# Norm products of q and k with a stationary tile of 128 columns in place of one of 16

## The chip, the cores and the metric

The kernel runs on one core of one Trainium2 chip. The metric is device time in microseconds, the median of repeated executions. TensorE is called PE below (PEld is its loading of stationary tiles), VectorE is DVE, ScalarE is ACT, GpSimd is POOL; SP is the engine whose queue issues nearly all DMAs here.

## The reference

Two kinds of layer alternate, attention (A) and a gated linear unit (B), twice each with the same weights, on x of 2048 tokens by 448 features; all is float32.

```python
def _A_ref(x, wqkv, wo):                 # H = 16 heads of Dh = 28
    qkv = transpose((x @ wqkv).reshape(B, S, 3, H, Dh), 2, 0, 3, 1, 4)
    q, k, v = qkv[0], qkv[1], qkv[2]
    scores = einsum("bhqd,bhkd->bhqk", q, k) * (Dh ** -0.5)
    o = einsum("bhqk,bhkd->bhqd", softmax(scores), v)
    return transpose(o, 0, 2, 1, 3).reshape(B, S, D) @ wo
def _B_ref(x, w_gate, w_up, w_down):     # F = 1792
    return (sigmoid(x @ w_gate) * (x @ w_up)) @ w_down

x = x + _A_ref(layernorm(x), wqkv, wo)
x = x + _B_ref(layernorm(x), w_gate, w_up, w_down)
x = x + _A_ref(layernorm(x), wqkv, wo)
x = x + _B_ref(layernorm(x), w_gate, w_up, w_down)
```

## The kernel before

The order of the instructions on every engine is the order in which the program writes them; no scheduler moves anything. x stays in SBUF. Products with weights are made of f16 parts: each float32 operand is split into a high and a low part, and a product is the sum of high by high, high by low and low by high.

Each of the two layers runs through projection, attention, output projection and gated unit. The change lies in the projection (`project`), which goes over four blocks of 512 tokens: for each block `qk` and then the values (`vals`); the blocks 2 and 3 have their `qk` first and their values after.

`qk(b, ...)` makes the 896 rows of q and k in seven tiles of 128 rows. For each tile i, eleven matmuls of 512 columns go into a PSUM bank (`by_features`, L362). ACT scales the sum to f16 (L506), DVE takes the low part (L507), ACT squares the high part into the bf16 tile `sq` (L509), DVE takes the larger of its first and second half of the columns (L511), SP stores both parts to DRAM (L514). Between these, the list `fill` gives each tile a piece of preparation for later blocks: layer norm, transposes on DVE, stores and gathers through DRAM (`store` L269, `gather` L277), splits into parts (`ready`, L172, L173, L177, L178). In layer 0 the weights are scaled and split along with the first block (`along`, L185, L188), and block 1 is transposed on PE (`turn`, L328) instead of through DRAM.

The norm products bound the scores. `ind` is a table of 8 tiles of [128, 16] in bf16: entry (p, i, h) is 1 where row p of a tile of q or k belongs to head h, else 0; the first four entries of i serve the tiles 0 to 3 for q, the second four the tiles 3 to 6 for k. A matmul of 256 columns with `ind[:, i, :]` as its stationary tile sums the squares of each head into 16 rows of a PSUM bank, `qnorm` for i up to 3 (L485) and `knorm` for i from 3 on (L488); the tile i = 3 holds rows of both and has two products. `sq` of tile i is not used at once: the products wait in `late` until two more tiles have had their matmuls, so those of tile 0 come after the matmuls of tile 2, and the last two tiles' products come in `finish`, which the code calls in the values that follow or in the next block. DVE then takes the largest of each head's row (L524, `peaks`). After block 3 a bound for every head comes of `peaks`, and from it a row that is added to the scores, and a flag (`guard_of_norms`, `worst_of_heads`).

Attention then works in tiles of 32 stationary columns at four places of the array (L821, L839). `ind` is written once at the start: POOL makes it in float32 (L150 to L156) and DVE copies it to bf16 (L159).

Of the kernel before, what the change touches and what calls it, by code (L numbers as in the profile page):

```python
# [12 lines left out]
BF16 = mybir.dt.bfloat16  # L13
# [6 lines left out]
P = 128  # L20
S = 2048
D = 448
H = 16
# [5 lines left out]
W = TB * P  # L29
# [54 lines left out]
def interleaved_layers(ctx: ExitStack, tc: tile.TileContext, x_in, wqkv, wo, w_gate, w_up,  # L84
                       w_down, out):
    nc = tc.nc
    ctx.enter_context(tc.manual_schedule())

    cpool = ctx.enter_context(tc.tile_pool(name="cpool", bufs=1))
# [26 lines left out]
    def bank(i, name):  # L116
        return psum(f"bank{i}", name, [P, 512])
# [4 lines left out]
    half = cpool.tile([P, 8], F32, name="half")  # L122
    nhalf = cpool.tile([P, TB], F32, name="nhalf")
    ind_f = qrt.get("ind_f", [P, 8, H])
    ind = cpool.tile([P, 8, H], BF16, name="ind")
    warm = cpool.tile([P, 1], F32, name="warm")

    ones = cpool.tile([P, P], F32, name="ones")
# [22 lines left out]
    for j in range(2):  # L151
# [4 lines left out]
        nc.gpsimd.affine_select(out=v, in_=v, compare_op=ALU.is_ge, fill=0.0,  # L156
                                base=DH - 1 - off, pattern=[[-P, 4], [DH, H]],
                                channel_multiplier=-1)
    nc.vector.tensor_copy(ind, ind_f)  # L159
    qrt.put(ind_f)  # L160


# [187 lines left out]
    def by_features(pm, blk, wh, wl, first_tile=None):  # L350

        order = [(wh, blk.hi), (wh, blk.lo), (wl, blk.hi)]
        terms = [(w(kt), x[:, kt, :]) for kt in range(3) for w, x in order]
        tails = [(w(3), blk.tail) for w in (wh, wl)]
        if first_tile == 0:
            terms = terms[0::3] + terms[2::3] + terms[1::3] + tails
        elif first_tile == 1:
            terms = terms[0::3] + terms[1::3] + tails[0:1] + terms[2::3] + tails[1:2]
        else:
            terms += tails  # L360
        for i, (w, x) in enumerate(terms):
            nc.tensor.matmul(pm, w, x, start=(i == 0), stop=(i == len(terms) - 1))  # L362
# [104 lines left out]
    def project(layer, wq, first):  # L467
# [11 lines left out]
        def qk(b, blk, fill, before):  # L479
            pn = [bank(4 + 2 * (b % 2), "qnorm"), bank(5 + 2 * (b % 2), "knorm")]  # L480
            late = deque()

            def norm_products(i, sq):
                if i <= 3:
                    nc.tensor.matmul(pn[0][0:H, 0:W // 2], ind[:, i, :], sq[:, 0:W // 2],  # L485
                                     start=(i == 0), stop=(i == 3))
                if i >= 3:
                    nc.tensor.matmul(pn[1][0:H, 0:W // 2], ind[:, 1 + i, :], sq[:, 0:W // 2],  # L488
                                     start=(i == 3), stop=(i == 6))
                qrt.put(sq)  # L490

            for i in range(7):
                pm = bank(evac[0] % 4, "qkp")
                evac[0] += 1
                c = slice(i * P, (i + 1) * P)
                by_features(pm, blk, lambda kt: wq.qk[0][:, kt, c],
                            lambda kt: wq.qk[1][:, kt, c], i if layer == 0 and b == 0 else None)
                if layer == 0 and b == 0:
                    along[i]()
                if i == 1 and before:  # L500
                    before()
                if len(late) == 2:
                    late.popleft()()
                hl = qrt.get("qkhl", [P, 2, W], F16)
                sq = qrt.get("sq", [P, W], BF16)
                nc.scalar.activation(hl[:, 0, :], pm, AF.Copy, scale=PS)  # L506
                nc.vector.scalar_tensor_tensor(hl[:, 1, :], pm, PS, hl[:, 0, :], op0=ALU.mult,  # L507
                                               op1=ALU.subtract)
                nc.scalar.activation(sq, hl[:, 0, :], AF.Square)  # L509

                nc.vector.tensor_tensor(sq[:, 0:W // 2], sq[:, 0:W // 2], sq[:, W // 2:W],  # L511
                                        op=ALU.max)
                n = slice(b * W, (b + 1) * W)
                nc.sync.dma_start(qk_scr[c, :, n], hl)  # L514
                qrt.put(hl)
                late.append(lambda i=i, sq=sq: norm_products(i, sq))
                if i < len(fill) and fill[i]:
                    fill[i]()

            def finish():  # L520
                while late:
                    late.popleft()()
                for i in range(2):
                    nc.vector.tensor_reduce(peaks[:, i, b:b + 1], pn[i][0:H, 0:W // 2], axis=AX.X,  # L524
                                            op=ALU.max)
            return finish
# [38 lines left out]
        sq = lambda b, *js: lambda: blks[b].squares(js)  # L565
# [19 lines left out]
        else:  # L585
# [4 lines left out]
            along_values = {0: b2.store, 3: lambda: b1.ready(3),  # L590
                            2: lambda: (b1.ready(0, 1, 2), fin(), b2.gather())}
        fin = qk(0, blks[0], fill, None)
        vals(0, blks[0], along_values)
        if layer == 0:
            fill = [b2.gather, b3.norm, sq(3, 0, 1), sq(3, 2, 3), idle,
                    lambda: b2.ready(0, 1), lambda: (b2.ready(2, 3), b3.store())]
        else:
            fill = [idle, b3.norm, lambda: b2.ready(0, 1), lambda: b2.ready(2, 3), sq(3, 0, 1),
                    sq(3, 2, 3), b3.store]
        fin = qk(1, b1, fill, None)  # L600
        vals(1, b1, {0: b3.gather, 1: fin})
        fin = qk(2, b2, [idle, lambda: b3.ready(0, 1), lambda: b3.ready(2, 3)], None)
        fin = qk(3, blks[3], [], fin)
        if layer > 0:
# [515 lines left out]
```

## Time and profile before

| | |
|---|---|
| three runs | 2023.3, 2023.67, 2027.02 us; median 2023.67 us |
| the profiled execution | 2026.13 us |
| its span, from the first to the last instruction | 2024.2 us |
| granted PE clock, mean | 0.998 |
| projection of layer 0 / layer 1 | about 17 to 129 us / 1020 to 1129 us of the span |
| norm products in the profile | 64, in 48 places of PE's stream |

A row of the time order reads: start in us, busy time in us, engine, line, operation, output<-inputs, shape of the stationary tile (rows\*columns), shape of the moving data and type, how many of them were merged; in brackets the idle time of the engine before it and what ended that. A row of a stretch reads: start:end, its length, then busy time and (xinstructions) of PE, PEld, DVE, ACT and POOL, the granted clock, the DMA share and GB/s. A row of a group reads: line, engine, operation, output<-inputs, shapes, count, then busy time in us, mean ns of one, idle time before them and what ended it. A row that gives durations as three numbers has least/median/most in ns. In the chain of work that ended last a row has start, time, engine, tile, line and count. SPq is the issuing queue of SP. Matmuls overlap, and their ends are modelled, so that distances are best taken from start to start.

### The profile page before, as it was taken

What the parts mean: (1) busy time and instruction counts of PE and PEld (TensorE: products, weight loads), DVE (VectorE), ACT (ScalarE), POOL (GpSimd) and SP (SyncE); (2) the same over time, 40 slices, a digit from 0 to 9 for tenths busy, and PEclk for the clock granted to TensorE, in tenths of its full rate; (3) what the DMA queues carried; (4) which work ended last, traced back from release to release, by engine and by line L of the source; (5) the groups of instructions that cost most, each with busy time, mean ns of one, the idle gap of its engine ahead of it and who ended that gap; (6) DMA issues with size and microseconds to landing.
All of it is one profiled execution on the core that took longest, in us unless ns stands there. A gap on an engine that the chain in (4) does not pass through costs nothing. (4 is left out here: it accounts for less than half of the span.)

```text
span 2024.2 us, 47829 instructions
## 1 busy us (share of the span) xinstructions
PE 2005.5 (99%) x21637; PEld 1028.8 (51%) x21637; DVE 748.8 (37%) x1110; ACT 1189.6 (59%) x1136; POOL 33.3 (2%) x75
## 2 busy tenths in 40 slices
PE   8999999999999999999999999999999999999999
PEld 4445555555554444444444555555555544444444
DVE  6635455551235232323274133222322432323222
ACT  5469999999961212121244799999999412121211
POOL 2000000000000000000000000000000000000000
PEclk9999999999999999999999999999999999999999
DMA  4563454741215100001143221121202250101000
GB/s 164 156 195 96 130 157 147 227 131 30 57 59 188 37 13 25 19 19 33 59 130 120 66 66 34 42 46 30 66 12 63 68 204 1 55 1 55 1 19 19
DMA packets 98630, 153.75 MB, mean 76 GB/s; under 512 B 9584, under 2 KB 79216, under 8 KB 95600
## 3 DMA queue, kind: packets, MB, share of 16 engines
q1 hardware_dynamic: 89728, 146.21, 23.9%
q10 hardware_dynamic: 8688, 4.36, 0.8%
q8 instruction: 174, 2.85, 0.6%
q14 instruction: 40, 0.33, 0.1%
HBM read 97.52 MB, written 45.68 MB: 71 GB/s over the span
## 5 line engine op out<-in xcount | busy, mean ns | idle before, releaser
L828 ACT ACTIVATE prob_s<-sc 128x1536 f32<-128x1536 f32 (+1 forms) x684 | 918.2, 1509 | 2.6 <-PE sc L821 1.4
L839 PE MATMUL acc<-prob_s,val_s 128*32 128x256 f32 x8192 | 571.7, 379 | 0.0
L821 PE MATMUL sc<-qp_s 114*32 114x512 f16 x8192 | 569.8, 380 | 1.5 <-ACT val_s L537 1.3
L362 PEld LDWEIGHTS <-gu_s 128*128 128x128 f16 x2464 | 241.1, 98 | 290.4 <-issue 6.4
L839 PEld LDWEIGHTS acc<-prob_s,val_s 128*32 128x32 f32 x8192 | 273.6, 110 | 179.8 <-ACT prob_s L828 0.4
L821 PEld LDWEIGHTS <-qp_s 114*32 114x32 f16 x8192 | 245.8, 95 | 222.3 <-issue 75.8
L362 PE MATMUL gate<-xhl_s,gu_s 128*128 128x512 f16 x1232 | 285.1, 379 | 4.2 <-ACT xhl_s L172 2.6
L362 PE MATMUL up<-xhl_s,gu_s 128*128 128x512 f16 x1232 | 284.2, 379 | 0.0
L1028 ACT ACTIVATE sig_q<-gate 128x512 f32<-128x512 f32 x112 | 66.9, 597 | 341.0 <-PE gate L362 324.8
L1033 DVE SCALAR_TENSOR_TENSOR sig_q<-up,sig_q 128x512 f32<-128x512 f32 x112 | 77.5, 692 | 460.9 <-PE up L362 460.9
L172 ACT CAST hhl_q<-sig_q 128x512 f16<-128x512 f32 x112 | 69.3, 618 | 288.1 <-DVE sig_q L1033 288.1
L853 DVE COPY oraw_q<-acc 128x512 f32<-128x512 f32 x32 | 22.1, 692 | 484.5 <-PE acc L839 484.4
L999 PE MATMUL dnp<-dn_s,hhl_q 128*128 128x448 f16 x448 | 157.9, 352 | 0.0
L998 PE MATMUL dnp<-dn_s,hhl_q 128*128 128x448 f16 x448 | 157.9, 352 | 0.0
L1000 PE MATMUL dnp<-dn_s,hhl_q 128*128 128x448 f16 x448 | 157.9, 352 | 0.0
L362 PE MATMUL qkp<-xhl_s,wqk_s 128*128 128x512 f16 x616 | 140.8, 380 | 0.9 <-DVE xhl_s L178 0.7
L855 DVE RECIPROCAL oden_q<-oden_q 128x512 f32<-128x512 f32 x32 | 107.3, 3353 | 1.1
L173 DVE TENSOR_TENSOR hhl_q<-sig_q,hhl_q 128x512 f16<-128x512 f32 x112 | 77.5, 692 | 76.7 <-ACT hhl_q L172 76.7
L362 PEld LDWEIGHTS <-wqk_s 128*128 128x128 f16 x616 | 57.2, 98 | 71.7 <-issue 4.5
L506 ACT ACTIVATE qkhl_q<-qkp 128x512 f16<-128x512 f32 x56 | 33.4, 596 | 65.5 <-PE qkp L362 65.4
L999 PEld LDWEIGHTS <-hhl_q 128*128 128x128 f16 x448 | 43.8, 98 | 43.8
L998 PEld LDWEIGHTS <-hhl_q 128*128 128x128 f16 x448 | 43.8, 98 | 43.8
(113 smaller groups left out, 1034.8 us busy)
## 6 DMA issues: line engine op xcount, KB each, us to landing
qp_s<-qk_scr SPq DMA_DIRECT2D x96, 224.0 KB
qk_scr<-qkhl_q SPq DMA_DIRECT2D x56, 256.0 KB
gu_s<-gu_parts SPq DMA_DIRECT2D x14, 1024.0 KB
xraw_s<-xt_scr SPq DMA_DIRECT2D x14, 768.0 KB
xt_scr<-xs_s SPq DMA_DIRECT2D x38, 224.0 KB
qp_s<-qk_scr SPq DMA_DIRECT2D x64, 112.0 KB
gu_parts<-pack_s SPq DMA_DIRECT2D x7, 1024.0 KB
raw_s<-in_B_w_down_dram SPq DMA_DIRECT2D x6, 896.0 KB
```

Source lines behind the costliest of these rows:

```text
L172: nc.scalar.copy(hi, raw)
L173: nc.vector.tensor_tensor(lo, raw, hi, op=ALU.subtract)
L362: nc.tensor.matmul(pm, w, x, start=(i == 0), stop=(i == len(terms) - 1))
L821: nc.tensor.matmul(ps[32 * j:32 * j + 32, a, :], hd.k[:, keys], hd.q[:, qb * W:(qb + 1) * W], start=True, stop=True, tile_position=(0, 32 ...
L828: nc.scalar.activation(prob[:, 0:n, :], ps[:, 0:n, :], AF.Exp, scale=exp_scale)
L839: nc.tensor.matmul(acc[qb * VC:(qb + 1) * VC, n], v[:, kc % TB, h, :], probs[c * NB + qb][:, n], start=(kc == 0 and i % 2 == 0), stop=(kc ...
L855: nc.vector.reciprocal(den, den)
L998: nc.tensor.matmul(pm, hl[:, 0, s], dw[:, 0, :], start=(f == 0), stop=False)
L999: nc.tensor.matmul(pm, hl[:, 0, s], dw[:, 1, :], start=False, stop=False)
L1000: nc.tensor.matmul(pm, hl[:, 1, s], dw[:, 0, :], start=False, stop=(f == NF - 1))
L1028: nc.scalar.activation(sig, pgu[0], AF.Sigmoid, scale=gate_scale)
L1033: nc.vector.scalar_tensor_tensor(sig, pgu[1], PS, sig, op0=ALU.mult, op1=ALU.mult)
```

## The change

`ind` gets seven more tiles of zeros behind its eight (POOL writes them at the start). The norm products take as their stationary tile the 128 columns that begin at tile i of the table, which are tiles i to i+7, in place of the 16 columns of tile i. They write 128 rows of the PSUM bank in place of 16. The first 16 rows are what was written before; the other 112 are sums over other tiles' heads, which nobody reads. The products are the same in number, place and moving data, and `peaks` still reads the first 16 rows. In the changed file the products stand at L490 and L493, the other lines of `project` move down by five.

```diff
-    ind = cpool.tile([P, 8, H], BF16, name="ind")
+    ind = cpool.tile([P, 7 + P // H, H], BF16, name="ind")
...
-    nc.vector.tensor_copy(ind, ind_f)
+    nc.gpsimd.memset(ind[:, 8:, :], 0.0)
+    nc.vector.tensor_copy(ind[:, 0:8, :], ind_f)
...
+            def rows_of_heads(i):
+
+                return ind[:, i:i + P // H, :].rearrange("p a h -> p (a h)")
+
             def norm_products(i, sq):
                 if i <= 3:
-                    nc.tensor.matmul(pn[0][0:H, 0:W // 2], ind[:, i, :], sq[:, 0:W // 2],
+                    nc.tensor.matmul(pn[0][:, 0:W // 2], rows_of_heads(i), sq[:, 0:W // 2],
                                      start=(i == 0), stop=(i == 3))
                 if i >= 3:
-                    nc.tensor.matmul(pn[1][0:H, 0:W // 2], ind[:, 1 + i, :], sq[:, 0:W // 2],
+                    nc.tensor.matmul(pn[1][:, 0:W // 2], rows_of_heads(1 + i), sq[:, 0:W // 2],
                                      start=(i == 3), stop=(i == 6))
                 qrt.put(sq)
```

## The prediction

> **What bounds the kernel now.** I read the page's busy shares first, then the stretches, the waits of PE, the order of time on PE and PEld around the products that change, and last what holds PE before and after them. The stretches are cut at the ends of the stages: layer 0's projection is the second row, layer 1's the third.
>
> ```profile
> span 2024.2 us, 47829 instructions
> ...
> PE 2005.5 (99%) x21637; PEld 1028.8 (51%) x21637; DVE 748.8 (37%) x1110; ACT 1189.6 (59%) x1136; POOL 33.3 (2%) x75
> 17.00:131.00 114.00, 111.21 (x556) 49.80 (x555) 69.08 (x142) 56.94 (x94) 6.50 (x10) 1.00 0.42 129
> 1020.00:1129.00 109.00, 106.84 (x508) 46.34 (x507) 63.54 (x134) 50.07 (x85) 5.89 (x8) 1.00 0.44 135
> ```
>
> PE is busy for 111.2 of 114 us and 106.8 of 109 us there, at the full granted clock (the 1.00): what leaves PE's stream shortens the span, unless PE must then wait. But busy hides gaps between pipelined matmuls, so I take the price of a product from starts, not durations.
>
> ```profile
> 100.84 2.55 PE L362 MATMUL qkp<-xhl_s,wqk_s 128*128 128x512 f16 x11
> 103.31 0.28 PE L485 MATMUL qnorm<-sq_q,ind 128*16 128x256 bf16 x1
> 103.52 2.55 PE L362 MATMUL qkp<-xhl_s,wqk_s 128*128 128x512 f16 x11
> 106.00 0.28 PE L485 MATMUL qnorm<-sq_q,ind 128*16 128x256 bf16 x1
> 106.21 2.55 PE L362 MATMUL qkp<-xhl_s,wqk_s 128*128 128x512 f16 x11
> 108.69 0.28 PE L485 MATMUL qnorm<-sq_q,ind 128*16 128x256 bf16 x1
> 108.80 0.27 PE L488 MATMUL knorm<-sq_q,ind 128*16 128x256 bf16 x1
> 109.01 2.55 PE L362 MATMUL qkp<-xhl_s,wqk_s 128*128 128x512 f16 x11
> ...
> 100.83 2.06 PEld L362 LDWEIGHTS <-wqk_s 128*128 128x128 f16 x11
> 103.31 0.09 PEld L485 LDWEIGHTS <-ind 128*16 128x16 bf16 x1 [0.42 <-issue]
> ...
> 1629.53 2.37 PE up L362 x11
> 1631.90 2.37 PE gate L362 x11
> ```
>
> Eleven 512-column matmuls with nothing between take 2.37 us (the last two rows, from the chain in order of time). Two products that follow each other stand 0.11 us apart (108.69 to 108.80). So eleven matmuls and one product should take 2.48 us. From 100.84 to 106.21 two such rounds take 5.37 us, 2.685 each: about 0.205 us more per visit. Of it some 0.10 us is on the way out: from 103.31 to 103.52 is 0.21, not 0.11; the rest is on the way in. The PEld rows show the same thing: among equal tiles a stationary load runs ahead of its matmul, but the load of `ind` starts in the instant its matmul starts, 0.42 us after the load before it. PE is emptied ahead of the product and once more behind it. A visit with two products pays this once: there are 64 products (32 of L485, 32 of L488), 16 visits hold two, so 48 visits, 24 in each layer.
>
> **The change, part by part.** (1) The 64 products get 128 stationary columns, the same shape as the matmuls around them. Is the price one of shape, or of the change from f16 to bf16? Nearest rows:
>
> ```profile
> 40.94 0.35 PE L369 MATMUL vp<-wv_s,xhl_s 128*128 128x448 f16 x1
> 41.13 1.04 PE L328 MATMUL turn<-ident,xn_s 128*128 128x128 f32 x8
> 42.00 0.35 PE L371 MATMUL vp<-wv_s,xhl_s 128*128 128x448 f16 x1
> ...
> 120.26 0.35 PE L369 MATMUL vp<-wv_s,xhl_s 128*128 128x448 f16 x1
> 120.54 0.20 PE L634 MATMUL bounds<-ident,bnd 16*1 16x16 f32 x2
> ```
>
> From f16 to f32 at 128*128 the step is 0.19 us, the plain distance of these matmuls: a change of type costs nothing. From `vp` to the 16*1 tile it is 0.28, 0.09 more. So shape carries the price, and I take it as gone: between 0 kept (as at 41.13) and 0.205 kept (were bf16 special), the first row is nearest, being again a change of type alone. A rule is weighed here. The Trainium skill, "TensorEngine Tiling (Array Packing)", section "Key Properties", says that changing the tiling mode drains TensorE, which the rows of the 16-column products bear out. But four of the eight transposes from 41.13 to 42.00 have 64 columns and all eight keep 0.11 us, so this trace does not show it for every narrow tile; by the rule taken word for word these would pay too.
>
> (2) The load. Its rows:
>
> ```profile
> L485 PEld LDWEIGHTS <-ind x32: 85/85/86, 24.5 to 1109.0; 128*16 128x16 bf16 x32
> L362 PEld LDWEIGHTS <-wqk_s 128*128 128x128 f16 x616 | 57.2, 98 | 71.7 <-issue 4.5 <-DVE wqk_s L188 0.7 <-ACT xhl_s L334 0.5
> ```
>
> 128 columns load in 98 ns, 16 in 85 ns. A product lasts 0.11 us, so the load of the next tile (98 ns) still fits beside it, barely. I charge nothing; if that cover is gone, at most 0.10 us a visit returns (rival 2).
>
> (3) The products write 128 PSUM rows and only the first 16 are read (L524): the moving side stays 256 columns, so no time. (4) POOL gets one more memset (128x112), and one stationary load a wait on it:
>
> ```profile
> 2.91 0.25 POOL L156 TENSOR_SCALAR_AFFINE_SELECT ind_f_q<-ind_f_q 128x64 f32<-128x64 f32 x1
> 9.49 0.19 POOL L318 TENSOR_SCALAR rs<-mv 128x1 f32<-128x1 f32 x1 [6.33 <-DVE mv L316]
> ```
>
> POOL then idles 6.33 us, and the first visit is 21 us later. Nothing queues behind it: zero. No DMA is added or moved.
>
> **What is given back.** 48 visits x 0.205 = 9.8 us leave PE's stream. PE arrives sooner, so I looked for places where it already waits for something that does not move.
>
> ```profile
> 26.35 1.82 DVE L188 SCALAR_TENSOR_TENSOR wqk_s<-wraw_s,up,wqk_s 128x1536 f16<-128x1536 f32 x1 [1.18 <-ACT wqk_s L185]
> 28.23 2.12 PE L362 MATMUL qkp<-xhl_s,wqk_s 128*128 128x512 f16 x9 [0.20 <-DVE wqk_s L188]
> 33.89 2.08 DVE L188 SCALAR_TENSOR_TENSOR wv_s<-wraw_s,up,wv_s 128x1792 f16<-128x1792 f32 x1
> 36.28 0.35 PE L372 MATMUL vp<-wv_s,xhl_s 128*128 128x448 f16 x1
> 54.61 0.27 PE L485 MATMUL qnorm<-sq_q,ind 128*16 128x256 bf16 x1 [0.73 <-DVE sq_q L511]
> 62.47 0.27 DVE L511 TENSOR_TENSOR sq_q<-sq_q 128x256 bf16<-128x256 bf16 x1
> 62.79 0.27 PE L485 MATMUL qnorm<-sq_q,ind 128*16 128x256 bf16 x1
> 65.42 0.27 DVE L511 TENSOR_TENSOR sq_q<-sq_q 128x256 bf16<-128x256 bf16 x1
> 65.74 0.27 PE L488 MATMUL knorm<-sq_q,ind 128*16 128x256 bf16 x1
> ```
>
> Layer 0: the two visits before 28.23 (0.41 us) are lost, since PE waits there for a weight split of DVE that hangs on ACT. Three more by 36.1 would give 0.6, but L372 needs the low part of `wv_s`, which DVE ends at 35.97: from 36.28 that leaves 0.31, less the 0.06 that PE takes to start after such an end (62.47+0.27 = 62.74 to 62.79 is 0.05): 0.25. From then to 65.74 DVE is packed with norms and squares; PE waits for it at 54.61, and the products at 62.79 and 65.74 start 0.05 us after DVE ends. DVE's row of work there starts from PE's transposes at 41.13, so it comes 0.25 sooner and no more; what the visits between save is waited away. The way out of the last one adds 0.10. From 65.9 on DVE has room, and 13 visits keep 13 x 0.205 = 2.67. Layer 0: 0.25 + 0.10 + 2.67 = 3.0 us.
>
> ```profile
> 1025.57 0.69 DVE L507 SCALAR_TENSOR_TENSOR qkhl_q<-qkp,qkhl_q 128x512 f16<-128x512 f32 x1 [0.91 <-ACT qkhl_q L506]
> 1032.82 3.48 SPq L269 DMA_DIRECT2D xt_scr<-xs_s  x4
> 1040.45 0.39 SPq L277 DMA_DIRECT2D xraw_s<-xt_scr  x1
> 1045.92 1.66 ACT L172 CAST xhl_s<-xraw_s 128x512 f16<-128x512 f32 x3 [2.73 <-DMA xraw_s<-xt_scr]
> 1049.89 5.34 PE L362 MATMUL qkp<-xhl_s,wqk_s 128*128 128x512 f16 x24 [0.69 <-DVE xhl_s L178]
> ```
>
> Layer 1: at 1049.89 PE waits for block 1's operands. Their chain is DVE's packed work from 1025.57 (before the first visit, at 1027.2), the store on SP, its landing, the gather, its landing, ACT, DVE. Nothing of it hangs on a visit, so the six visits before it (1.2 us) only lengthen this wait. The 18 after it keep 18 x 0.205 = 3.7 us. What follows in both layers (guard, loads of heads, attention) starts from the last products and moves with PE.
>
> Sum: 3.0 + 3.7 = 6.7 us. The profiled execution took 2026.13 us (span 2024.2 and 1.93 around it), 2.46 above the median of the three runs, 2023.67. 2026.13 - 6.7 = 2019.4; on the median, 2023.67 - 6.7 = **2017.0 us**, 0.33% less.
>
> **Rivals.** 1: no wait holds PE back, as the release points move too; then all 48 visits count: 2023.67 - 9.8 = 2013.9. For it: many of DVE's steps are themselves started by PE; against it, the chain to 1049.89, with two DMA landings.
> 2: the next load doesn't fit under a 0.11 us product and half the price stays: the 31 visits that count (13 + 18) give 31 x 0.105 = 3.3, with 0.25 from the start 3.5: 2020.2. For it: 98 ns of some 110. Against it: at 42.00 a 128*128 load follows a 0.11 us matmul with no extra distance.
> 3: the price is not of shape (of bf16, or of `ind`) and nothing changes: 2023.7. Against it: the rows at 41.13 and 120.54.
> 4, slower: the 128-column stationary, read as overlapping rows, loads much longer than 98 ns in the emptied array, on PE's path at each product. It decides once a load is 0.205 us longer than 85 ns, thus beyond 290 ns; the longest kind in the trace needs 230:
>
> ```profile
> L400 PEld LDWEIGHTS sums<-sums,ones 128*128 128x128 f32 x6 | 1.3, 230 | 3.9 <-POOL rs L318 3.6
> ```
>
> Were the price of shape kept and the load 230 ns, 64 x 0.145 = 9.3 us: 2033. With the load of 98 ns and the price kept it is 64 x 0.013 = 0.8 us, 2024.5, within the bound. The Trainium skill, "TensorE: Matmul & The Clock Gate", section "LDWEIGHTS (loading the stationary operand)", speaks for this rival: the load goes by columns alone, columns / 1.2 ns; an estimate from it is 13 ns for 16 and 107 ns for 128, with the price kept 64 x 0.094 = 6.0 us, 2029.7. The rows say 85 and 98.
>
> **How the numbers follow.** Forecast (2017.0, for itself 2015.5 to 2018.5) 0.64, rival 1 0.11, rival 2 0.12, rival 3 0.08, rival 4 0.05. A measurement can tell about 0.2% (4.0 us) from no change: below 2019.6 is faster. The forecast and rival 1 lie there, rivals 2 and 3 within the bound, rival 4 above. The three runs spread 3.7 us, so the forecast's 6.7 may measure a little less at times, and rival 2 a little more: faster 0.76, same 0.19, slower 0.05. The range takes in rivals 1 and 2 and leaves out 3 and 4: 2013.5 to 2020.8.
>
> **What would show it.** Products of form 128*128 at L490 and L493; a round of 2.48 instead of 2.685 us; no idle time of PEld before `ind`; the wait before block 1 of layer 1 grown from 0.69 by about 1.2 us; the first score matmul of each layer earlier by 3.0 and 6.7 us. Rounds still at 2.6 or more would make me wrong, as would a second layer no sooner than 2 us or a new wait after 66 us.

## The result, and the profile after

The changed kernel takes 2014.05 us (median of six runs, 2013.51 to 2016.58) against 2024.4 us of the kernel before in the same count of runs (2023.3 to 2027.02). The ratio is 0.9948, with a 95% interval of 0.9935 to 0.9961: 10.35 us less. The forecast was 6.7 us less, 2017.0 us; the time lies in the stated range, 0.55 us above its lower end, and below the 2015.5 to 2018.5 that the forecast claimed for itself.

The page of the changed kernel, then its time order on PE and on PEld at the place the prediction showed (its lines lie a little lower in the file: L363 is the old L362, L490 and L493 are the norm products):

```profile
span 2012.1 us, 47832 instructions
PE 1994.3 (99%) x21637; PEld 1032.1 (51%) x21637; DVE 749.0 (37%) x1110; ACT 1189.6 (59%) x1136; POOL 33.2 (2%) x76
...
96.31 2.54 PE L363 MATMUL qkp<-xhl_s,wqk_s 128*128 128x512 f16 x11
98.69 0.27 PE L490 MATMUL qnorm<-sq_q,ind 128*128 128x256 bf16 x1
98.80 2.54 PE L363 MATMUL qkp<-xhl_s,wqk_s 128*128 128x512 f16 x11
101.17 0.27 PE L490 MATMUL qnorm<-sq_q,ind 128*128 128x256 bf16 x1
101.28 1.03 PE L363 MATMUL qkp<-xhl_s,wqk_s 128*128 128x512 f16 x4
...
96.20 2.15 PEld L363 LDWEIGHTS <-wqk_s 128*128 128x128 f16 x11
98.47 0.10 PEld L490 LDWEIGHTS <-ind 128*128 128x128 bf16 x1
```

A round takes 2.485 us (96.31 to 101.28 is two of them, 4.97), where it took 2.685. The step from a product to the next matmul is 0.11 us, and the load of `ind` now starts 0.22 us ahead of its matmul (98.47, 98.69): the array is no longer emptied. That much is the forecast to the hundredth. But the round explains only a part. These starts bound the stages that changed: second `sums` to first score matmul in layer 0, first `op` to first `gate`, and in layer 1 first `qkp` to first score matmul; the fourth stage is first `op` to first `gate` in layer 1. First the kernel before, then the changed one:

```profile
21.92 0.28 PE L400 MATMUL sums<-sums,ones 128*128 128x1 f32 x2
...
128.94 1.26 PE L821 MATMUL sc<-qp_s 114*32 114x512 f16 x20 [0.63 <-ACT val_s L537]
...
591.11 0.36 PE L371 MATMUL op<-wout_s,ot_s 128*128 128x448 f16 x1
...
625.67 0.38 PE L362 MATMUL gate<-xhl_s,gu_s 128*128 128x512 f16 x1 [1.09 <-ACT xhl_s L172]
...
1019.99 7.29 PE L362 MATMUL qkp<-xhl_s,wqk_s 128*128 128x512 f16 x33
...
1129.01 1.26 PE L821 MATMUL sc<-qp_s 114*32 114x512 f16 x20 [0.63 <-ACT val_s L537]
```

```profile
19.48 0.28 PE L401 MATMUL sums<-sums,ones 128*128 128x1 f32 x2
...
123.55 0.61 PE L826 MATMUL sc<-qp_s 114*32 114x512 f16 x6 [0.63 <-ACT val_s L542]
...
585.97 0.36 PE L372 MATMUL op<-wout_s,ot_s 128*128 128x448 f16 x1
...
619.59 0.38 PE L363 MATMUL gate<-xhl_s,gu_s 128*128 128x512 f16 x1 [0.16 <-ACT xhl_s L173]
...
1013.91 7.29 PE L363 MATMUL qkp<-xhl_s,wqk_s 128*128 128x512 f16 x33
...
1117.30 1.48 PE L826 MATMUL sc<-qp_s 114*32 114x512 f16 x24 [0.63 <-DMA qp_s<-qk_scr]
```

The differences of these starts, with those of the further profiles that the experiments gave (all in us, each worked out from the same starts of its own profile):

| stage | before | before_again | after | after_again | after_third | pad_only | shift32 |
|---|---|---|---|---|---|---|---|
| projection, layer 0 | 107.02 | 107.17 | 104.07 | 104.23 | 103.66 | 107.21 | 104.12 |
| output projection to gate, layer 0 | 34.56 | 34.44 | 33.62 | 33.38 | 33.51 | 33.54 | 34.14 |
| projection, layer 1 | 109.02 | 108.12 | 103.38 | 103.47 | 103.75 | 108.13 | 105.33 |
| output projection to gate, layer 1 | 34.94 | 35.29 | 34.50 | 34.87 | 34.83 | 34.57 | 35.33 |
| sum | 285.54 | 285.02 | 275.57 | 275.95 | 275.75 | 283.45 | 278.92 |

Layer 0's projection lost 3.1 us (forecast 3.0). Layer 1's lost 5.0 (forecast 3.7), and 1.0 us left the output projection of layer 0, where there is no norm product at all. Another 2.4 us of the first profile lies ahead of the first row: the second `sums` come at 21.92 and at 19.48.

### The profile page after: what moved, and what is told of

Its sections match the earlier page's. It is cut to its first block, busy times and chain, and to the rows that moved or that the text cites. A ratio compares the mean times of both kernels' runs of the same rounds, so it can differ in the third digit from the quotient of the medians.

```text
span 2012.1 us, 47832 instructions
## 1 busy us (share of the span) xinstructions
PE 1994.3 (99%) x21637; PEld 1032.1 (51%) x21637; DVE 749.0 (37%) x1110; ACT 1189.6 (59%) x1136; POOL 33.2 (2%) x76
## 3 DMA queue, kind: packets, MB, share of 16 engines
q1 hardware_dynamic: 89728, 146.21, 23.1%
## 5 line engine op out<-in xcount | busy, mean ns | idle before, releaser
L363 PEld LDWEIGHTS <-gu_s 128*128 128x128 f16 x2464 | 241.1, 98 | 289.0 <-issue 5.0
L363 PE MATMUL gate<-xhl_s,gu_s 128*128 128x512 f16 x1232 | 285.1, 379 | 2.8 <-DVE xhl_s L174 1.4
L363 PE MATMUL up<-xhl_s,gu_s 128*128 128x512 f16 x1232 | 284.2, 379 | 0.0
L363 PE MATMUL qkp<-xhl_s,wqk_s 128*128 128x512 f16 x616 | 139.1, 379 | 0.8 <-DVE wqk_s L189 0.6
L363 PEld LDWEIGHTS <-wqk_s 128*128 128x128 f16 x616 | 60.1, 98 | 70.0 <-issue 1.9
```

## The experiments

**Is the unexpected part chance?** Both kernels once more, unchanged, one profile each.

> The kernel before, unchanged, for one more profile. Between the first two profiles the changed one starts its first norm product 2.53 us earlier, which no norm product can cause, and the trip of block 1 of layer 1 through DRAM (from the start of its stores at 1032.82 to the first cast of ACT at 1045.92, 13.10 us before, 11.36 us after) is 1.74 us shorter. Theory A (chance: DMA landings differ between executions): this profile shows other values than the first one, a first product between 22 and 25 us and a trip between 11.3 and 13.1 us. Theory B (the change speeds the trip up): the trip is again 13.0 to 13.2 us. The round of eleven matmuls and one product stays 2.685 us under both.

> The changed kernel, unchanged, for one more profile. Theory A (chance): the trip of block 1 of layer 1 lies anywhere from 11.3 to 13.1 us and the first product anywhere from 22 to 25 us. Theory B: the trip is again about 11.4 us. A round is 2.48 us.

Measured: 2023.03 and 2014.4 us, beside 2023.34 of the kernel before. The start is chance: in `before_again` the first product comes at 22.28 us and in `after_again` at 22.45, so the late start of the first profile belonged to that execution. The trip through DRAM is not. From the start of block 1's stores to the first cast of ACT, as the expectations have it, it takes 13.10 and 12.47 us in the two profiles of before and 11.36 and 11.06 in those of after. It varies by more than theory B allowed, but the two kernels stay apart. Its first part varies less: from the start of the stores to the start of the gather (below: store to gather) it takes 7.63 and 7.43 us before, 6.47 and 6.45 after. The page's row of the main DMA queue also differs, with the same packets and bytes (before, then after):

```profile
q1 hardware_dynamic: 89728, 146.21, 23.9%
```

```profile
q1 hardware_dynamic: 89728, 146.21, 23.1%
```

The same DMAs take less time; the pages of the two further profiles have 23.9 and 23.4%. So neither theory A as written (all chance) nor the products alone explain the gain; something in the change makes transfers faster. One row that the prediction read belonged to its execution too: `before_again` has no wait of PE before block 1 of layer 1, where the first profile has 0.69 us, and its projection of layer 1 is 0.9 us shorter (108.12 against 109.02).

**Which shapes pay?** The changed kernel with fewer columns:

```diff
-                return ind[:, i:i + P // H, :].rearrange("p a h -> p (a h)")
+                return ind[:, i:i + 4, :].rearrange("p a h -> p (a h)")     # cols64; cols112: 7
...
-                    nc.tensor.matmul(pn[0][:, 0:W // 2], rows_of_heads(i), sq[:, 0:W // 2],
+                    nc.tensor.matmul(pn[0][0:64, 0:W // 2], rows_of_heads(i), sq[:, 0:W // 2],
```

> Stationary tile of 64 columns (four tiles of the table), 64 rows of PSUM written. Theory A (every tile narrower than 128 empties the array): a round of 2.68 us, time near 2024 us. Theory B (only the 32-column tiles pay, as the 64-column transposes cost nothing extra in the trace of before): a round of 2.48 us, time near 2014 us.

> Stationary tile of 112 columns (seven tiles of the table): the shape of the array stays that of the matmuls around, but the tile is not full. Theory A (the price is one of the array's shape alone): a round of 2.48 us, time near 2014 us. Theory B (a load is fast only for 128 columns, and a slow one shows behind a product of 0.11 us): the load lasts well over 98 ns (150 to 170 if it goes with the columns as from 16 on) and the round is 2.53 to 2.56 us, so that 48 visits give back 2.4 to 3.8 us.

Time order on PE and the row of the loads, first with 64, then with 112 columns (the loads' three numbers are least, median and most in ns):

```profile
99.20 2.55 PE L363 MATMUL qkp<-xhl_s,wqk_s 128*128 128x512 f16 x11
101.68 0.30 PE L490 MATMUL qnorm<-sq_q,ind 128*64 128x256 bf16 x1
101.91 2.55 PE L363 MATMUL qkp<-xhl_s,wqk_s 128*128 128x512 f16 x11
...
L490 PEld LDWEIGHTS <-ind x32: 106/106/106, 22.7 to 1105.5; 128*64 128x64 bf16 x32
```

```profile
97.77 2.54 PE L363 MATMUL qkp<-xhl_s,wqk_s 128*128 128x512 f16 x11
100.14 0.27 PE L490 MATMUL qnorm<-sq_q,ind 128*112 128x256 bf16 x1
100.25 2.54 PE L363 MATMUL qkp<-xhl_s,wqk_s 128*128 128x512 f16 x11
...
L490 PEld LDWEIGHTS <-ind x32: 129/130/132, 23.2 to 1098.3; 128*112 128x112 bf16 x32
```

With 64 columns the round is 2.71 us here, and 2.68 at some other places: the price is there, as high as with 16 columns or a little higher (0.23). With 112 it is 2.48 us, as with 128, although the load takes 130 ns instead of 98: that load hides behind the matmul before it. In the rounds theory A holds in both. The rule of the Trainium skill, "TensorEngine Tiling (Array Packing)", section "Key Properties", that changing the tiling mode drains TensorE, fits the products of 16 and 64 columns, which pay; the 64-column transposes, which cost nothing extra, remain unexplained. The times, 2022.1 and 2014.41 us, say one thing more: with the full price, `cols64` is still 1.2 us below the kernel before. Its trip is the short one of the changed kernel (store to gather 6.51 us), which the table's size, the same in both, will explain.

**Is the price paid per product or per visit?** The kernel before, with the products done in twos:

```diff
-                if len(late) == 2:
+                if len(late) == 3:
+                    late.popleft()()
                     late.popleft()()
```

> The kernel before, tiles in their old places and 16 columns, but the products wait until three tiles are due and then two are done at once: 24 visits instead of 48, with the same 64 products. Theory A (the price is paid per visit, by the change of shape): a round with no product takes 2.37 us and one with two about 2.80; three visits a block leave, of which 6 in layer 0 and 9 in layer 1 count, 15 x 0.205 = 3.1 us, with up to 4.9 if nothing is waited away. Theory B (the price is that of each product): no gain, a round with two products 3.0 us.

```profile
96.34 4.92 PE L362 MATMUL qkp<-xhl_s,wqk_s 128*128 128x512 f16 x22
101.19 0.39 PE L485 MATMUL qnorm<-sq_q,ind 128*16 128x256 bf16 x2
101.51 4.92 PE L362 MATMUL qkp<-xhl_s,wqk_s 128*128 128x512 f16 x22
```

22 matmuls and two products take 5.17 us (96.34 to 101.51). Without a price they would be 2 x 2.37 + 2 x 0.11 = 4.96, so 0.21 us is paid, once for the two. The ratio to before is 0.9979 (0.9970 to 0.9989): 24 visits fewer give back 4.2 us by the ratio (2.2 to 6.1), between the 3.1 and the 4.9 that were expected; in the profile the two projections are 1.7 and 1.1 us shorter than the means of before. The price is one of the visit, by the change of shape.

**What made the transfers faster?** The table's tile grew by 224 bytes in each partition, and everything allotted behind it in SBUF moved up by as much. The big tiles, which the DMAs read and write, are taken to have lain 288 bytes past a multiple of 512 before and to lie on one after. That is a sum of the sizes of the tiles ahead of them: no trace shows an address, and only the distances between the layouts follow from the edits (224 bytes from before to after). `pad_only` moves the tiles in the kernel before; `shift32` moves them off again in the changed one.

```diff
# pad_only, from the kernel before
-    ind = cpool.tile([P, 8, H], BF16, name="ind")
+    ind = cpool.tile([P, 15, H], BF16, name="ind")
...
-    nc.vector.tensor_copy(ind, ind_f)
+    nc.vector.tensor_copy(ind[:, 0:8, :], ind_f)
# shift32, from the changed kernel (shift128: 11, shift256: 15)
-    ind = cpool.tile([P, 7 + P // H, H], BF16, name="ind")
+    ind = cpool.tile([P, 8 + P // H, H], BF16, name="ind")
```

> The kernel before with its 16-column products, but the table's tile allotted 15 entries instead of 8 (the seven more are never written or read), so that all big tiles behind it in SBUF lie 224 bytes higher, as in the changed kernel: they then begin at a multiple of 512 bytes, before 32 bytes past a multiple of 64. Theory A (the place of the tiles sets how long the trips through DRAM take): from the first matmul of the output projection to the first of the gated unit in layer 0 33.4 to 33.6 us (34.4 to 34.6 in two profiles of before), from the start of block 1's stores to its gather in layer 1 6.3 to 6.5 us (7.4 and 7.6), the wait of 0.7 us before block 1 of layer 1 gone; time 1.5 to 2.5 us below the kernel before. Theory B (the place is no matter): all as in the kernel before, time within 0.5 us of it. Rounds stay at 2.685 us.

> The changed kernel with one more unused entry of 32 bytes in the table's tile, so that the big tiles lie 32 bytes past a multiple of 64 again, with the 128-column products. Theory A: the trips are those of before (34.4 to 34.6 and 7.4 to 7.6 us), and the wait before block 1 of layer 1 grows as the prediction said, to a distance of 1.6 to 2.2 us between two starts; the projection of layer 1 takes 104.4 to 105.3 us, and the time is 1.5 to 3 us above that of the changed kernel, 6.5 to 8 below the kernel before. Theory B: as the changed kernel, about 2014.

The chain of block 1 in layer 1, first of the changed kernel (SP's queue, ACT, PE), then of `pad_only`, then of `shift32`:

```profile
1026.74 2.81 SPq L270 DMA_DIRECT2D xt_scr<-xs_s  x4
...
1033.20 0.39 SPq L278 DMA_DIRECT2D xraw_s<-xt_scr  x1
...
1038.10 1.66 ACT L173 CAST xhl_s<-xraw_s 128x512 f16<-128x512 f32 x3 [2.01 <-DMA xraw_s<-xt_scr]
...
1042.07 2.75 PE L363 MATMUL qkp<-xhl_s,wqk_s 128*128 128x512 f16 x12 [0.23 <-DVE xhl_s L179]
```

```profile
1029.70 2.84 SPq L269 DMA_DIRECT2D xt_scr<-xs_s  x4
1036.07 0.39 SPq L277 DMA_DIRECT2D xraw_s<-xt_scr  x1
...
1041.04 1.66 ACT L172 CAST xhl_s<-xraw_s 128x512 f16<-128x512 f32 x3 [0.96 <-DMA xraw_s<-xt_scr]
...
1043.91 7.29 PE L362 MATMUL qkp<-xhl_s,wqk_s 128*128 128x512 f16 x33
```

```profile
1027.00 3.50 SPq L270 DMA_DIRECT2D xt_scr<-xs_s  x4
1034.62 0.39 SPq L278 DMA_DIRECT2D xraw_s<-xt_scr  x1
...
1040.37 1.66 ACT L173 CAST xhl_s<-xraw_s 128x512 f16<-128x512 f32 x3 [4.02 <-DMA xraw_s<-xt_scr]
...
1041.04 0.38 PE L363 MATMUL qkp<-xhl_s,wqk_s 128*128 128x512 f16 x1 [0.89 <-ACT xhl_s L173]
1041.77 1.89 PE L363 MATMUL qkp<-xhl_s,wqk_s 128*128 128x512 f16 x8 [0.35 <-DVE xhl_s L174]
1044.34 5.34 PE L363 MATMUL qkp<-xhl_s,wqk_s 128*128 128x512 f16 x24 [0.69 <-DVE xhl_s L179]
```

On the trips theory A holds on both sides. With the old products and the new place, store to gather takes 6.37 us (1029.70 to 1036.07), and PE does not wait before block 1 (33 matmuls in one row at 1043.91). This last is no proof, as `before_again` has no wait there either, and its projection of layer 1 is as long (108.12 against 108.13). The ratio to before is 0.9978 (0.9968 to 0.9987). With the new products and a bad place the trip takes 7.62 us, and PE waits 0.89 + 0.35 + 0.69 = 1.9 us for block 1, against 0.23, 0 and 0.28 in the three profiles of the changed kernel; layer 1's projection takes 105.33 us, 1.8 more than the mean of the changed kernel's three profiles. Output projection to gate in layer 0 came out at 34.14 us, better than the 34.4 to 34.6 that were named. The ratio is 0.9959 (0.9945 to 0.9973).

Of the 1.1 us between a short and a long way to the gather, 0.7 lies in the issuing of the four stores on SP (2.81 and 2.84 us against 3.50). The trace's packets show the place as well: the stores' 1792 packets of 512 bytes took 31.6 to 31.9 ns on average in the three profiles of after and in `pad_only`, 34.9 to 35.5 in the two of before and in `shift32`.

From the table's sums, against the mean of the two profiles of before (285.28): the place alone gives 1.8 us (`pad_only`), the products alone 6.4 (`shift32`), both together 9.5 (mean of the three profiles of after, 275.76). The 1.3 us over 1.8 + 6.4 lie in layer 1's projection (0.4 and 3.2 apart, 5.0 together): with the slow trip, PE waits away what the first six visits saved; with the fast one it hardly has to wait. The sizes are rough, since the two profiles of before differ by 0.9 us in that stage.

The times split the gain otherwise. By the ratios the place alone is worth 4.5 us (2.6 to 6.5), which is more than the 1.5 to 2.5 that theory A named, and the products alone 8.3 (5.5 to 11.1). `pad_only` and `shift32` ran on another chip than `before_again`, and no profile of the kernel before was taken beside them; where the rest of the 4.5 us lies stays open. That the place counts is shown, how much of the 10 us it brings is not.

**Which places are good?** The changed kernel with the tiles 128 and 256 bytes past a multiple of 512:

> The changed kernel with the big tiles at 128 bytes past a multiple of 512. Theory A (a multiple of 512 is needed, as 192 past it was slow in the merged kernel): store to gather 7.4 to 7.6 us, output projection to gated unit 34.1 to 34.6. Theory B (a multiple of 128 is enough): 6.3 to 6.5 and 33.4 to 33.6.

> The changed kernel with the big tiles at 256 bytes past a multiple of 512. Theory A (a multiple of 512 is needed): 7.4 to 7.6 and 34.1 to 34.6 us. Theory B (a multiple of 128 or of 256 is enough): 6.3 to 6.5 and 33.4 to 33.6 us.

```profile
1027.11 3.24 SPq L270 DMA_DIRECT2D xt_scr<-xs_s  x4
1034.12 0.39 SPq L278 DMA_DIRECT2D xraw_s<-xt_scr  x1
...
1040.52 1.66 ACT L173 CAST xhl_s<-xraw_s 128x512 f16<-128x512 f32 x3 [4.06 <-DMA xraw_s<-xt_scr]
```

```profile
1028.42 2.84 SPq L270 DMA_DIRECT2D xt_scr<-xs_s  x4
1034.74 0.39 SPq L278 DMA_DIRECT2D xraw_s<-xt_scr  x1
...
1040.04 1.66 ACT L173 CAST xhl_s<-xraw_s 128x512 f16<-128x512 f32 x3 [2.27 <-DMA xraw_s<-xt_scr]
```

At 128 store to gather takes 7.01 us, at 256 6.32; at 32 (`shift32`) 7.62, at 288 (before) 7.4 to 7.6, at 192 (`merged_aligned`, below) 7.47. To the gather, then, 128 is about half way. To the first cast of ACT it is not: 13.41 us at 128 (1027.11 to 1040.52) and 13.37 at 32, against 11.62 at 256 and 11.06 to 11.40 in the changed kernel. The projection of layer 1 agrees, with 105.67 us at 128 and 103.88 at 256, and so does the main DMA queue's share on the pages: 23.1 to 23.4% at multiples of 256, 23.9 to 24.4% everywhere else, 128 included. So a multiple of 256 is as good as one of 512, and 128 is not enough. Output projection to gate in layer 0 lies between what the theories named, 33.89 us at 128 and 33.75 at 256.

Both single times, 2016.62 and 2016.47 us, lie above the changed kernel's median; for 256 the start accounts for it, as its first product comes at 23.92 us, 1.5 to 1.9 us later than in the profiles of the changed kernel.

The Trainium skill, "DMA: Bandwidth & Descriptors", section "How a descriptor splits into AXI transactions", has a descriptor that doesn't begin at a multiple of 256 bytes fetched from the boundary below, in pieces that begin at such multiples. As an estimate from that page, 512 bytes then cost 17 beats of 32 bytes at 32 past, 20 at 128 and 22 at 192, against 16. The stores' packets of 512 bytes come in this order (35.5, 37.0 and 41.0 ns on average, against 31.6 to 32.1 at multiples of 256), the whole trips don't. That this split is the cause of the longer trips, no run here shows.

**A version beyond both?** One table of 32 columns an entry, heads of q in the first 16 and of k in the last 16, gives one product for each of the seven tiles of a block:

```diff
-                if i <= 3:
-                    nc.tensor.matmul(pn[0][:, 0:W // 2], rows_of_heads(i), sq[:, 0:W // 2],
-                                     start=(i == 0), stop=(i == 3))
-                if i >= 3:
-                    nc.tensor.matmul(pn[1][:, 0:W // 2], rows_of_heads(1 + i), sq[:, 0:W // 2],
-                                     start=(i == 3), stop=(i == 6))
+                nc.tensor.matmul(pn[:, 0:W // 2], rows_of_heads(i), sq[:, 0:W // 2],
+                                 start=(i == 0), stop=(i == 6))
...
+            nc.vector.stream_shuffle(top[:, 1:2], top[:, 0:1], [(i + H) % 32 for i in range(32)])
```

> The changed kernel with one table of 32 columns an entry, heads of q in the first 16 and of k in the last 16, read as 128 columns (four entries): one product for each tile, 7 a block instead of 8, into one bank, and one maximum instead of two; at the end the rows of k are moved to those of q by one shuffle on DVE. Big tiles at a multiple of 64 bytes. Theory A (a product of equal shape costs 0.11 us and nothing else): 8 products fewer, 0.9 us less than the changed kernel, about 2013.2; theory B (the products fit beside other work by now): no difference.

It took 0.9961 of the kernel before (0.9948 to 0.9973), no better than the changed kernel: a multiple of 64 was not enough, the trip took 7.47 us. With 96 columns a product and three small tiles folded together the big tiles lie on a multiple of 512, and the changed kernel ran beside it:

> The changed kernel, unchanged, beside the next one on the same chip: about 0.995 of the kernel before, as in its first runs (0.9935 to 0.9961).

> One product for each tile as in the merged kernel, with three entries (96 columns) a product, and three small tiles folded together so that the big tiles begin at a multiple of 512 bytes again. Theory A (7 products of 0.11 us a block instead of 8, and fast trips through DRAM): the projection from the sums of the second third of the weights to the first score matmul 103.5 us (104.1 in the changed kernel), store to gather 6.3 to 6.5 us, time 0.8 to 1.2 us below the changed kernel on the same chip. Theory B: the trips stay at 7.5 us as in the first merged kernel, and the time 1 to 2 us above the changed one.

Both give 0.9942 of the kernel before (0.9928 to 0.9956 and 0.9929 to 0.9956), medians 2014.06 and 2014.11 us. Theory A's stage and trip came out (103.56 and 6.51 us, and the round with 96 columns is 2.48 us), its 0.8 to 1.2 us did not. In the profile layer 1's projection is 103.03 us against 103.38 to 103.75, so 4 products there give some 0.4 to 0.7 us, and layer 0's 103.56 against 103.66 to 104.23; that is too little to show in the time. Neither beats the other.

## Why the prediction was right, and what it missed

*The price of a visit*, 0.205 us, and that it would go entirely: right. The round fell from 2.685 to 2.485 us; `pairs16` shows that it is paid per visit, `cols64` and `cols112` that shape decides. The type never mattered, as products and table stayed bf16. So rival 3 fell, and with it rival 2: at a product of 0.11 us even a load of 130 ns stays hidden.

*Rival 4* (a long load): the load is 98 ns, as in the row it was judged by, and nothing of it reached PE's path.

*What is given back in layer 0*, 3.0 us: right, 3.1 measured (means of 107.1 and 104.0), and the places too. PE waits in the changed kernel where it was said to, for two weight splits first and then for the norms and squares on DVE, and nowhere later in this stage:

```profile
25.79 2.12 PE L363 MATMUL qkp<-xhl_s,wqk_s 128*128 128x512 f16 x9 [0.61 <-DVE wqk_s L189]
33.58 0.35 PE L373 MATMUL vp<-wv_s,xhl_s 128*128 128x448 f16 x1 [0.17 <-DVE wv_s L189]
59.99 0.27 PE L490 MATMUL qnorm<-sq_q,ind 128*128 128x256 bf16 x1 [0.57 <-DVE sq_q L516]
62.94 0.27 PE L493 MATMUL knorm<-sq_q,ind 128*128 128x256 bf16 x1 [0.20 <-DVE sq_q L516]
```

The first of these waits was 0.20 us before, and has grown by the 0.41 of the two visits ahead of it; the other three the profiles of before don't show.

*What is given back in layer 1*, 3.7 us: measured 5.0. The step that failed is "Nothing of it hangs on a visit, so the six visits before it (1.2 us) only lengthen this wait". It holds as far as it goes: the stores start 12.83 us after the projection's first matmul in the kernel before (1019.99 to 1032.82) and in the changed one (1013.91 to 1026.74). But the trip behind them was taken as fixed and became some 1.1 us shorter to the gather, so that the wait, named as a sign at 0.69 + 1.2 us, is 0.23 us. In `shift32`, where the trip is the old one, PE waits 1.9 us, as was said, and the stage took 105.33 us. That is the 3.7 us less than the first profile of before, and 2.8 less than the second, in which PE did not wait there.

*The sum* 6.7 us: the products alone gave 6.4 (`shift32` against the profiles of before), and 5.5 to 11.1 by its times. The other 3 us of the profiles come from the sentences "(4) POOL gets one more memset" and "No DMA is added or moved", which counted the bigger table as one memset and saw no more in it. No DMA moved in order, but the address of every big tile did. The first rival named the right time, 2013.9, by a wrong reason: all 48 visits were to count, and in layer 0 they did not; in layer 1 the operands came sooner, but by the addresses and not by the visits. That the time lies in the stated range is partly luck: the range had been drawn down to 2013.5 for that rival, and the gain that the sum left out just fits in.

## What to carry to other kernels

A small matmul of another array shape in a stream of full ones costs its two changes of shape, here 0.2 us per visit however many products are done in it: fill the stationary tile up with columns that nobody reads (a tile of 96 columns was enough here, one of 64 was not), or do several at one visit. Take the price from the distance of starts and from whether the load runs ahead, not from busy time. When a change alters the size of any tile, look at where the tiles allotted behind it come to lie: run the new layout with the old work, before the gain is put down to the work.

## What was not expected of the hardware

The place of tiles in SBUF sets the time of their DMAs: four stores to DRAM and the landing take 6.3 to 6.5 us when the tiles begin at a multiple of 256 bytes (by the sum of tile sizes), and 7.4 to 7.6 us at 32, 192 or 288 bytes past a multiple of 512, 7.0 at 128; that alone, with no instruction's work altered, was worth 0.22% of the time (`pad_only`, 0.13 to 0.32%). And a load of 112 columns takes longer (130 ns) than one of 128 (98 ns), while 64 take 106 and 16 take 85 (all bf16). By the Trainium skill, "TensorE: Matmul & The Clock Gate", section "Weight-path perf modes — Fast Weight Load (FWL) and DoubleRow", the quick path is for exactly 128 columns that are not float32, which these four agree with.
